# Key products of chunks 16 to 23 made ahead of the chunk loop, from inputs without block-diagonal copies

## The chip, the cores and the metric

The kernel runs on one core of one Trainium2 chip. The metric is the device time of one execution in microseconds. Before the change three executions took 909.39, 907.27 and 908.71 us, median 908.71 us. Below, PE is TensorE, DVE is VectorE, ACT is ScalarE, POOL is GpSimd and SP the engine that issues the DMAs.

## The reference, cut to what matters

Three layers follow one another: a delta-rule attention, a Fourier-mixing layer with an MLP, and a gated MLP. Only the attention is touched.

```python
def _attn_ref(q, k, v, beta):                 # (4, 8, 768, 48)
    k_n = k / (np.linalg.norm(k, axis=-1, keepdims=True) + 1e-06)
    state = np.zeros((B, H, D, D))
    for t in range(S):
        kt, vt, bt = k_n[:, :, t], v[:, :, t], beta[:, :, t, None]
        y[:, :, t] = np.einsum('bhd,bhde->bhe', q[:, :, t], state)
        v_old = np.einsum('bhde,bhd->bhe', state, kt)
        state = state + bt[:, :, :, None] * np.einsum('bhd,bhe->bhde', kt, vt - v_old)
```

## The kernel before, in words

The 768 steps are cut into chunks of C = 64, so that there are 48 pairs of batch and chunk (NBC = 48, numbered bc in the order in which they are worked on). A chunk covers 8 heads, held as 4 head pairs (HP) with one head on partitions 0 to 47 and the other on partitions 64 to 111. Eight chunks make a block (NB = 6 blocks).

For each chunk **stage_a** multiplies keys by queries and keys: the tile `kq` (112 x 4 x 256, 448 KB) holds, per head pair, 64 query columns, 64 key columns and 128 columns of keys once more, laid out block-diagonally, so that one whole-array matmul (L204) serves both heads. The products are evicted from a PSUM bank (tag X, 4 banks) into the ring tile `gak`. For chunks 8 to 15 ACT evicts in three instructions without the causal mask (L186, L187, L208); for chunks 16 on DVE evicts and masks in one (L210). Chunks 0 to 7 have a form of their own, `pairs0` (L178): keys and queries come without the block-diagonal copy, and each head is a matmul of 48 rows by 64 columns, one head in one corner of the array and one in the other.

**prep** (L233 to L243) builds from the key products of a block the triangular system that **solve** inverts on DVE (L253 to L308, mostly L287 and L292). `prep(blk + 1)` stands inside `solve(blk)` and waits in program order until stage_a has been recorded for the whole next block. For block 1 prep multiplies by a mask of its own (L238), since its products were evicted unmasked; `mask_q` (L220, L224) masks the query part of such chunks later, two chunks at a time.

The program has a **head** and a **chunk loop**. In the head: fills, 20 small warm-up matmuls (`busy`, L473, which compute nothing that is used), `pairs0` for keys, `solve(0)` on DVE, `pairs0` for queries, stage_a for chunks 8 to 15 each followed by one 512-column `busy` matmul (`keep`), then 8 more (`last`), `mask_q(0)` and `start(1)`, which is prep and root of block 1. The loop runs t from -3 to 47. Iteration t merges half-blocks of the inverse (`merge`, L359 and L362, 32x32 matmuls, evicted by ACT as `zs` and `TT`), and calls stage_b(t + 2) (L393, evicted into `WU`), stage_c(t + 1) (L409, then DVE's `cw`, L410) and stage_d(t) (L422, L424, then ACT's `Sb` and `x`). It also calls stage_a for a chunk 20 ahead (`ring`): chunks 16 and 17 at t = -3, 18 and 19 at t = -2 and -1, then t + 20. The instructions of `solve` are spread over eight iterations between those calls.

Instructions run in the order in which they are recorded on each engine; `chain` ties this order down. So an instruction that waits holds back all that follows on its engine, and the engines wait for each other in the order of the program.

Of the kernel before, what the change touches and what calls it, by code (L numbers as in the profile page):

```python
# [7 lines left out]
F32 = mybir.dt.float32  # L8
# [12 lines left out]
C = 64  # L21
NC = S // C
HP = H // 2
NBC = B * NC
# [3 lines left out]
GA = C + 2 * D  # L28
NT = B * S // 128

TOK = np.concatenate([np.arange(S // 2), [S // 2], S - np.arange(1, S // 2)])

MG = [(0, 97), (97, 193), (193, 289), (289, 384)]
# [8 lines left out]

CF = dict(
    skew=4, ring=20, kq=5, qt=3, mb=2, cvd=3, cve=2, kn=4, sv="hhhhhd", few=3,
    warm=20, keep=1, last=8, cuts=(0.5, 0.65), dfs=(1, 1, 1, 1, 2, 2, 3, 1, 1, 1, 2), cvt=(0, 0, 0, 0, 1, 1, 1, 1, 1, 1, 1), early=5,
    turns=(4, 5, 6, 7, 8, 9, 10, 11, 13, 14, 15, 16, 17, 17, 18, 19), stats=(((0, 1, 2, 3, 3), (2,)), ((20, 21, 22), (23, 24, 25))),
)

# [14 lines left out]
class Kernel:  # L63
# [36 lines left out]
    def load(self, out, in_):  # L100
        return self.nc.sync.dma_start(out=out, in_=in_)
# [13 lines left out]
    def attention(self, cp, pg, pe, p, x, filler, after_solves):  # L115
        nc, a, load = self.nc, self.a, self.load
# [12 lines left out]
        gas, Tts, st, kqs, qts, preps, seen_a = {}, {}, {}, {}, {}, {}, [0]  # L129
# [32 lines left out]
        def ring(bc):  # L162

            gak = (pe if bc // 4 % 6 < 3 else p).tile([128, 4, HP, GA], F32, name="gak", bufs=3)
            for i in range(4):
                gas[bc + i] = gak[:, i]
            gas[bc, 4] = gak


        ROWS = (slice(0, D), slice(0, C)), (slice(64, 64 + D), slice(64, 64 + C))  # L170
# [10 lines left out]
        def both0(i, at):  # L181
            return gas[i // 2 * 4, 4][:, i % 2 * 2 : i % 2 * 2 + 2, :, at : at + C].rearrange("p a b c -> p (a b) c")

        def copy_g(out, in_):

            nc.scalar.activation(out[:, :, :32], in_[:, :, :32], AF.Copy, scale=mk[:, 4 * C + 1 : 4 * C + 2])  # L186
            nc.scalar.copy(out=out[:, :, 32:], in_=in_[:, :, 32:])  # L187

        def mask_a(bc, n):
            m = 2 * C if SEQ[bc][1] < HALF else 0  # L190
            return mk[:, m : m + n].unsqueeze(1)

        def load_kq(bc):
            if 8 <= bc < NBC:
                kqs[bc] = pe.tile([112, HP, 4 * C], F32, name="kq", bufs=CF["kq"])
                load(out=kqs[bc], in_=a["kq"][bc])

        def stage_a(bc):
            kq = kqs.pop(bc)
            if bc % 4 == 0:  # L200
                ring(bc)
            pa = self.bank("pa", [128, HP, 2 * C])
            for hp in range(HP):
                nc.tensor.matmul(pa[:, hp], lhsT=kq[:, hp, 2 * C :], rhs=kq[:, hp, : 2 * C], start=True, stop=True)  # L204
            if bc < 16:

                copy_g(gas[bc][:, :, C : 2 * C], pa[:, :, C:])
                nc.scalar.copy(out=gas[bc][:, :, :C], in_=pa[:, :, :C])  # L208
            else:
                nc.vector.tensor_tensor(  # L210
                    out=gas[bc][:, :, : 2 * C], in0=pa, in1=mask_a(bc, 2 * C).to_broadcast([128, HP, 2 * C]), op=MUL
                )
            load_kq(bc + CF["kq"])
            seen_a[0] = bc + 1

        def mask_q(bc):
# [10 lines left out]
        def prep(blk):  # L227


            Cc = pe.tile([128, 1024], F32, name="Cc").rearrange("p (g c) -> p g c", g=32)  # L230
            for h4 in range(2):
                g4 = gas[blk * 8 + h4 * 4, 4][:, :, :, C : 2 * C].rearrange("p a b c -> p (a b) c")
                nc.vector.scalar_tensor_tensor(  # L233
                    out=Cc[:, h4 * 16 : h4 * 16 + 16], in0=g4[:, :, 32:], scalar=mk[:, 4 * C : 4 * C + 1], in1=g4[:, :, :32], op0=MUL, op1=ADD
                )
                yield 750
            if blk == 1:
                nc.vector.tensor_mul(Cc, Cc, mk[:, 4 * C + 2 : 4 * C + 34].unsqueeze(1).to_broadcast([128, 32, 32]))  # L238
                yield 1200

            Tf = pe.tile([128, 1056], F32, name="Ts", bufs=CF["mb"])
            T = Tf[:, :1024].rearrange("p (i j) -> p i j", i=32)
            nc.vector.transpose(out=T, in_=Cc.rearrange("p g c -> p c g"))  # L243
            preps[blk] = Tf, T
            yield 2000
# [85 lines left out]
        def start(blk):  # L331
            for _ in prep(blk):
                pass
            root(blk)
# [37 lines left out]
        def load_kv(bc):  # L372
            load(out=gas[bc][:, :, C:], in_=a["kv"][bc])
# [70 lines left out]
        for n in "kq":  # L444
            t = p.tile([128, 4, HP, GA], F32, name="gak", bufs=3).rearrange("p a b c -> p (a b c)")[:112, :2048]
# [4 lines left out]
                load(out=bt, in_=a["bt"])  # L450
                load(out=mk, in_=a["mk"])
        for i in range(CF["kq"]):
            load_kq(8 + i)
        load(out=qx, in_=a["qx"].rearrange("b p h -> p b h"))
        for i in range(2):
            load_qt(i)
# [11 lines left out]
        warm = TT[0].rearrange("p a b -> p (a b)")  # L468

        def busy(n, cols):  # L470
            wb = self.bank("pd", [128, cols])
            for i in range(n):
                nc.tensor.matmul(wb, lhsT=warm[:, :128], rhs=warm[:, :cols], start=True, stop=True)  # L473
# [8 lines left out]
        Spread(solve(0), 0).finish()  # L482
        for i in range(4):
            nc.scalar.copy(out=both0(i, 0), in_=pairs0("q", i))
        for bc in range(8, 16):
            stage_a(bc)
            busy(CF["keep"], 512)
        busy(CF["last"], 512)
        mask_q(0)
        start(1)  # L490
# [6 lines left out]
        R = CF["ring"]  # L497
        T0 = -3
        for t in range(T0, NBC):
            j, i = divmod(t + 11, 8)  # L500
            if i == 0 and j < NB:
                if solver:
                    solver.finish()
                solver = Spread(solve(j), 27600 if j < NB - 1 else 29000)
            part = (lambda f: solver.upto((i + f) / 8)) if j < NB else (lambda f: None)
            if light(t) and solver:
                solver.finish()
                solver = None

            if 0 <= t + 2 < NBC:  # L510
                values(t + 2)
            if t % 2 == 0 and 2 <= t + 2 < 16:
                mask_q(t + 2)
            part(c1)
            if t >= 0:
                stage_d(t)
                if SEQ[t][1] == NC - 1:
                    fill.extend(filler(SEQ[t][0]))
            new = t % 8 == 5 and t + 3 < NBC
            if new:  # L520

                merge((t + 3) // 2, True, False)
                load_kv(t + 3)
                load_kv(t + 4)
                diag((t + 3) // 2, up)
            if 0 <= t + 1 < NBC:
                stage_c(t + 1)
            part(c2)
            if t + R < NBC:
                if t >= 0:  # L530
                    stage_a(t + R)
            if t % 2:
                g = (t + 3) // 2
                if g < NBC // 2:
                    merge(g + 1, (g + 1) % 4 > 0, True)
                    if new:
                        diag(g, lo)
            elif t % 8 != 4 and t + 4 < NBC:
                diag((t + 4) // 2, up + lo)
            if (t + 4) % 8 > 1 and t + 4 < NBC:  # L540
                load_kv(t + 4)
            if light(t):

                for _ in range(CF["dfs"][t - (NBC - 11)]):
                    while fill and next(fill[0], 1) == 1:
                        fill.pop(0)
                for _ in range(CF["cvt"][t - (NBC - 11)]):
                    next(tail, None)
            if 0 <= t + 2 < NBC:
                stage_b(t + 2)  # L550
            if 2 <= t + 4 < NBC:
                load_qt(t + 4)
            if t < 0:
                for bc in range(16 if t == T0 else t + R, t + R + 1):
                    stage_a(bc)
            part(1)
            self.chain()
            if t == NBC - 12:
                loads, tail = after_solves()
            next(loads, None)  # L560
            self.chain()
# [536 lines left out]
def layout(q, k, v, beta, moe_w_ch1, moe_w_ch2, moe2_w_in, moe2_w_spatial, moe2_b_spatial, moe2_w_out):  # L1098
    f = np.float32
    o = {}  # L1100
# [11 lines left out]
    kq = np.zeros((B, NC, 2, 64, HP, 4, C), f)  # L1112
# [4 lines left out]
    kq = kq.reshape(NBC, 128, HP, 4 * C)[perm, :112]  # L1117
    o["kq"] = kq

    o["kq0"] = np.stack([kq[:8, :, :, C : 2 * C], kq[:8, :, :, :C]]).transpose(0, 2, 1, 3, 4)  # L1120

    qe = np.zeros((B, NC, 2, 64, HP, 112), f)
# [10 lines left out]
    j, i = (np.arange(128) % C)[:, None], np.arange(C)[None]  # L1133
# [7 lines left out]
    r = [np.arange(j, S // 2, 6)[None] for j in range(6)]  # L1141
# [39 lines left out]
    o["wi"] = rows(moe2_w_in)  # L1181
    o["ws"] = rows(moe2_w_spatial.T[np.ix_(TOK, TOK)])
    o["wo"] = rows(moe2_w_out)
    o["bs"] = moe2_b_spatial[TOK].reshape(1, S)
    return {n: np.ascontiguousarray(w) for n, w in o.items()}
# [19 lines left out]
```

## Time and profile before

| what | value |
|---|---|
| median of 3 executions | 908.71 us (907.27 to 909.39) |
| the profiled execution | 907.29 us, its span 905.5 us |
| busy PE / DVE / ACT | 863.4 us (95%) / 596.1 us (66%) / 392.0 us (43%) |
| chain that ended last, by engine | PE 72%, DVE 17%, ACT 8% |
| mean granted TensorE clock | 0.98 of full speed |

Busy shares are averages over the whole span. [...] The chain is followed back from the last instruction and says what each step waited for.

### The profile page before, as it was taken

The numbers are of one execution on the slowest core, as the hardware profiler recorded it, in microseconds if no ns is written. First come the engines' busy times: TensorE is split into PE (matmuls) and PEld (weight loads), VectorE is DVE, ScalarE is ACT, GpSimd is POOL, SyncE is SP. The second block draws the span as 40 slices with busy tenths as digits, with TensorE's granted clock in tenths as the row PEclk, the third lists the DMA queues.
The fourth block names the chain that finished last, engine by engine and source line by source line (L and its number), as shares of the span: only waits on it lengthen the run. The fifth ranks groups of instructions, "written<-read, shape, count | busy, mean of one in ns | idle before, by whom it ended". The sixth has DMA issues, their size and how long they took to land.

```text
span 905.5 us, 18349 instructions
## 1 busy us (share of the span) xinstructions
PE 863.4 (95%) x7115; PEld 826.0 (91%) x7115; DVE 596.1 (66%) x1796; ACT 392.0 (43%) x1004; POOL 71.2 (8%) x75
## 2 busy tenths in 40 slices
PE   7969999999999798999999999999999999999998
PEld 7668888998899688999999999999989999899898
DVE  5989999898875999678393694422385472452521
ACT  1265878788966544311212252221262251341412
POOL 2000000000000000000000000000023222222221
PEclk8988999999999999999999999999999999999999
DMA  7565565642354360000011511110132210000001
GB/s 213 163 164 130 147 183 155 167 133 72 90 152 128 97 234 1 1 1 11 17 46 52 167 27 27 27 27 18 31 110 70 73 34 27 28 1 27 27 1 54
DMA packets 58698, 70.88 MB, mean 78 GB/s; under 512 B 31953, under 2 KB 49074, under 8 KB 58610
## 3 DMA queue, kind: packets, MB, share of 16 engines
q1 hardware_dynamic: 58610, 69.70, 26.9%
q8 instruction: 56, 0.92, 0.4%
q14 instruction: 32, 0.26, 0.1%
HBM read 57.29 MB, written 4.72 MB: 68 GB/s over the span
## 4 chain that ended last, share of the span: by engine, by line
PE 72%; DVE 17%; ACT 8%; issue 2%; DMA 1%; POOL 0%; ACTq 0%; SPq 0%; DVEq 0%; POOLq 0%
PE bankX L791 15%; PE bankY L807 13%; PE bankX L930 11%; PE bankX L916 6%; PE bankY L950 6%; PE bankX L891 5%; DVE tm L287 2%; DVE Ts L292 2%; PE bankY L409 2%; ACT TT L348 2%; PE bankY L393 2%; ACT WU L398 2%; PE bankY L424 2%; PE bankX L612 2%; PE bankY L422 2%
## 5 line engine op out<-in xcount | busy, mean ns | idle before, releaser
L791 PE MATMUL bankX<-uh,w 128*128 128x384 f32 x504 | 136.8, 338 | 2.4 <-DVE ul L719 2.4
L807 PE MATMUL bankY<-w,hh 128*128 128x384 f32 x504 | 117.5, 339 | 1.1 <-DVE w L693 1.1
L799 DVE SCALAR_TENSOR_TENSOR hl<-bankX,hh 128x384 fp32r<-128x384 f32 x84 | 46.4, 552 | 97.2 <-ACT hh L798 97.2
L798 ACT ACTIVATE hh<-bankX 128x384 fp32r<-128x384 f32 x84 | 41.2, 491 | 156.9 <-PE bankX L791 154.6
L930 PE MATMUL bankX<-ws,vh 128*128 128x384 f32 x384 | 97.6, 336 | 0.0
L791 PEld LDWEIGHTS bankX<-uh,w 128*128 128x128 f32 x504 | 91.9, 188 | 3.1 <-DVE ul L719 2.9
L807 PEld LDWEIGHTS bankY<-w,hh 128*128 128x128 f32 x504 | 90.1, 188 | 2.2 <-DVE w L693 1.7
L791 PE MATMUL bankX<-ul,w 128*128 128x384 f32 x252 | 84.9, 337 | 0.0
L422 PE MATMUL bankY<-WU,gak 128*112 128x96 f32 (+1 forms) x384 | 70.2, 271 | 3.5 <-ACT x L439 3.2
L424 PE MATMUL bankY<-Sb,cw 112*112 112x96 f32 (+1 forms) x352 | 66.0, 271 | 7.9 <-DVE cw L410 6.4
L908 POOL TENSOR_TENSOR vl<-v,vh 128x512 fp32r<-128x512 f32 x24 | 31.9, 1335 | 519.1 <-DMA x<-un 442.4
L807 PE MATMUL bankY<-w,hl 128*128 128x384 f32 x252 | 72.1, 338 | 0.0
L930 PEld LDWEIGHTS bankX<-ws,vh 128*128 128x128 f32 x384 | 69.4, 188 | 0.0
L938 DVE TENSOR_TENSOR g<-bankX,bsb 128x384 f32<-128x384 f32 x32 | 17.7, 557 | 78.2 <-PE bankX L930 71.9
L930 PE MATMUL bankX<-ws,vl 128*128 128x384 f32 x192 | 63.7, 336 | 0.0
L292 DVE TENSOR_TENSOR Ts<-Ts,tm 128x110 f32<-128x110 f32 (+26 forms) x264 | 59.0, 261 | 0.8
L287 DVE TENSOR_TENSOR tm<-Ts 128x110 f32<-128x110 f32 (+26 forms) x264 | 58.7, 259 | 0.5
L424 PEld LDWEIGHTS bankY<-Sb,cw 112*112 112x112 f32 (+1 forms) x352 | 50.8, 184 | 8.5 <-issue 6.1
L422 PEld LDWEIGHTS bankY<-WU,gak 128*112 128x112 f32 (+1 forms) x384 | 54.2, 184 | 4.6 <-ACT x L439 4.3
L393 PE MATMUL bankY<-gak,TT 128*128 128x96 f32 x384 | 54.1, 286 | 3.2 <-issue 2.7
L393 PEld LDWEIGHTS bankY<-gak,TT 128*128 128x128 f32 x384 | 48.7, 198 | 5.2 <-issue 3.0
L916 PE MATMUL bankX<-xh,s 128*128 128x384 f32 x192 | 50.1, 338 | 1.4 <-ACT v L900 1.4
(179 smaller groups left out, 1858.8 us busy)
## 6 DMA issues: line engine op xcount, KB each, us to landing
kq<-in_kq_dram SPq DMA_DIRECT2D x40, 448.0 KB, 4.2
qt<-in_qt_dram SPq DMA_DIRECT2D x48, 196.0 KB, 3.9
gak<-in_kv_dram SPq DMA_DIRECT2D x48, 192.0 KB, 3.9
w<-in_w_dram SPq DMA_DIRECT2D x24, 384.0 KB, 7.5
x<-un SPq DMA_DIRECT2D x128, 36.0 KB, 1.9
out_dram<-ot SPq DMA_DIRECT2D x24, 192.0 KB, 2.0
s<-in_wi_dram SPq DMA_DIRECT2D x6, 512.0 KB, 4.5
un<-xh SPq DMA_DIRECT2D x80, 36.0 KB, 1.9
```

The lines of the kernel that those rows point to most:

```text
L287: nc.vector.tensor_tensor(out=tm, in0=T[:, r, k : k + 1].to_broadcast(sh), in1=T[:, k : k + 1, :k].to_broadcast(sh), op=MUL)
L292: nc.vector.tensor_add(o, o, tm)
L393: nc.tensor.matmul(pb[:, hp].rearrange("p t d -> p (t d)"), lhsT=tt[:, o + hp], rhs=kv[:, hp], start=True, stop=True)
L422: nc.tensor.matmul(pd[:m, hp], lhsT=ak[:, hp, :m], rhs=u[:, hp], start=True, stop=(c == 0))
L424: nc.tensor.matmul(pd[:m, hp], lhsT=cw[:, hp, :m], rhs=sb[:, hp], start=False, stop=True)
L791: nc.tensor.matmul(ph, lhsT=w1[f][i][:, c * 128 : c * 128 + 128], rhs=cur[k][:, c], start=(c + j == 0), stop=(c == 2 and j == 2))
L799: nc.vector.scalar_tensor_tensor(out=hl, in0=ph, scalar=0.0, in1=hh.bitcast(F32), op0=MAX, op1=SUB)
L807: nc.tensor.matmul(acc[t], lhsT=hx[i][:, t * 128 : t * 128 + 128], rhs=w2[e][k], start=(e == 0 and j == 0), stop=(e == 11 and j == 2),)
L891: nc.tensor.matmul(pv, lhsT=xT[t // 3][i][:, c, (t % 3) * 128 : (t % 3) * 128 + 128], rhs=wi[2 * c + 1][k], start=(c + j == 0), stop=(c == ...
L916: nc.tensor.matmul(pu, lhsT=wi[2 * c][i][:, f * 128 : f * 128 + 128], rhs=xT[hf][k][:, c], start=(c + j == 0), stop=(c == 2 and j == 2),)
L930: nc.tensor.matmul(pv, lhsT=vn[i][:, s, f * 128 : f * 128 + 128], rhs=ws[2 * s + hf][k], start=(s + j == 0), stop=(s == 5 and j == 2),)
L950: nc.tensor.matmul(po, lhsT=gt[i][:, f, t * 128 : t * 128 + 128], rhs=wo[f][k], start=(f + j == 0), stop=(f == 3 and j == 2),)
```

## The change

Chunks 8 to 23 (HEAD = 24) now all have their stage_a in the head. Their input is a new array `kc` without the block-diagonal copies: one `kq` tile of 448 KB holds two chunks. Each head pair is two matmuls of 48 rows by 64 columns (`ROWS`, as in `pairs0`) in place of one whole-array matmul. ACT evicts all of them unmasked. The `keep` matmuls are gone and `last` is 16 in place of 8. The loop's stage_a begins at t = 4 with chunk 24; the masks follow, for block 2's keys in `prep` (one multiplication of 128x1024) and for the queries of chunks 16 to 23 in `mask_q` at t = 14, 16, 18 and 20.

```diff
+HEAD = 24
-    warm=20, keep=1, last=8, ...
+    warm=20, keep=1, last=16, ...
         def load_kq(bc):
-            if 8 <= bc < NBC:
+            if bc < HEAD:
+                if 8 <= bc and bc % 2 == 0:
+                    t = pe.tile([112, HP, 4 * C], F32, name="kq", bufs=CF["kq"]).rearrange("p a n -> p (a n)")
+                    kqs[bc], kqs[bc + 1] = (t[:, i * HP * 2 * C : (i + 1) * HP * 2 * C].rearrange("p (a n) -> p a n", a=HP) for i in range(2))
+                    load(out=t.rearrange("p (c n) -> p c n", c=2), in_=a["kc"][:, bc - 8 : bc - 6])
+            elif bc < NBC:
...
             for hp in range(HP):
-                nc.tensor.matmul(pa[:, hp], lhsT=kq[:, hp, 2 * C :], rhs=kq[:, hp, : 2 * C], start=True, stop=True)
-            if bc < 16:
+                if bc < HEAD:
+                    for r, q in ROWS:
+                        nc.tensor.matmul(pa[q, hp], lhsT=kq[r, hp, C:], rhs=kq[r, hp], start=True, stop=True)
+                else:
+                    nc.tensor.matmul(pa[:, hp], lhsT=kq[:, hp, 2 * C :], rhs=kq[:, hp, : 2 * C], start=True, stop=True)
+            if bc < HEAD:
...
-            if blk == 1:
+            if blk in (1, 2):
                 nc.vector.tensor_mul(Cc, Cc, mk[:, 4 * C + 2 : 4 * C + 34].unsqueeze(1).to_broadcast([128, 32, 32]))
...
-        for bc in range(8, 16):
+        for bc in range(8, HEAD):
             stage_a(bc)
-            busy(CF["keep"], 512)
         busy(CF["last"], 512)
...
-            if t % 2 == 0 and 2 <= t + 2 < 16:
+            if t % 2 == 0 and 2 <= t + 2 < HEAD:
                 mask_q(t + 2)
...
-            if t + R < NBC:
-                if t >= 0:
-                    stage_a(t + R)
+            if HEAD <= t + R < NBC:
+                stage_a(t + R)
+            if t < T0 + CF["kq"]:
+                load_kq(HEAD + t - T0)
...
-            if t < 0:
-                for bc in range(16 if t == T0 else t + R, t + R + 1):
-                    stage_a(bc)
```

The order on PE from the program's start to the first stage_b, before the change; `TT` is the operand of the `busy` matmuls, `kq` the input of stage_a, bankZ what `merge` writes, and the row with bankY<-gak is the first stage_b:

```order
L473 MATMUL bankY<-TT_83 128x128 x20
L178 MATMUL bankX<-gak 64x64 x128
L204 MATMUL bankX<-kq 128x128 x4
L473 MATMUL bankY<-TT_83 128x512
...
L473 MATMUL bankY<-TT_83 128x512 x9
L359 MATMUL bankZ<-T_406,gak 32x32 x17
L362 MATMUL bankZ<-TT_83,zs 32x32
...
L204 MATMUL bankX<-kq 128x128 x8
L393 MATMUL bankY<-gak,TT_83 128x96 x4
```

The same place on PE with the change (line numbers are those of the changed kernel):

```order
L488 MATMUL bankY<-TT_83 128x128 x20
L180 MATMUL bankX<-gak 64x64 x128
L213 MATMUL bankX<-kq 64x128 x128
L488 MATMUL bankY<-TT_83 128x512 x16
L374 MATMUL bankZ<-T_406,gak 32x32 x17
L377 MATMUL bankZ<-TT_83,zs 32x32
...
L408 MATMUL bankY<-gak,TT_83 128x96 x4
```

Between the 128 small matmuls of `pairs0` and the first merge PE now has 128 more small matmuls and 16 `busy` matmuls in one piece, where it had 8 times 4 whole-array matmuls with a `busy` matmul behind each and 8 more at the end; the 8 matmuls of chunks 16 and 17 ahead of the first stage_b are gone.

The order on DVE at the end of `solve(1)` (t = 3 and 4), before the change; `T` and `Tc` are the inverse, `Cc` and the second `Ts` the system of block 2, `sq` its diagonal:

```order
L294 TENSOR_TENSOR Ts<-Ts,dT 128x1024
L410 TENSOR_TENSOR cw<-qt,bankY 112x448
L300 STREAM_TRANSPOSE T_1082<-Ts 128x512
L210 TENSOR_TENSOR gak<-bankX,mk 128x4x128
L300 STREAM_TRANSPOSE T_1082<-Ts 128x512
L410 TENSOR_TENSOR cw<-qt,bankY 112x448
L210 TENSOR_TENSOR gak<-bankX,mk 128x4x128
L233 SCALAR_TENSOR_TENSOR Cc<-gak,mk 128x512 x2
L243 STREAM_TRANSPOSE Ts<-Cc 128x1024
L220 TENSOR_TENSOR gak<-gak,mk 128x8x64
L308 STREAM_TRANSPOSE Tc<-Ts 128x16x32
L136 COPY sq<-Ts 128x32
```

The same place on DVE with the change:

```order
L309 TENSOR_TENSOR Ts<-Ts,dT 128x1024
L425 TENSOR_TENSOR cw<-qt,bankY 112x448
L315 STREAM_TRANSPOSE T_1154<-Ts 128x512 x2
L248 SCALAR_TENSOR_TENSOR Cc<-gak,mk 128x512 x2
L425 TENSOR_TENSOR cw<-qt,bankY 112x448
L253 TENSOR_TENSOR Cc<-Cc,mk 128x1024
L258 STREAM_TRANSPOSE Ts<-Cc 128x1024
L235 TENSOR_TENSOR gak<-gak,mk 128x8x64
L323 STREAM_TRANSPOSE Tc<-Ts 128x16x32
L221 TENSOR_TENSOR gak<-bankX,mk 128x4x128
L138 COPY sq<-Ts 128x32
```

The evictions of chunks 22 and 23 are gone, the mask of block 2's system has come in, and the eviction of chunk 24 stands one instruction earlier. The building of that system no longer comes behind the eviction of chunk 23.

## Rows read from the trace of the kernel before

**Rows 1.** The page's first line.

```profile
span 905.5 us, 18349 instructions
```

**Rows 2.** The chain that ended last, 43 to 72 us: start, length, step.

```profile
48.40 0.20 DVE sq L136
...
48.85 0.27 ACT zs L365
...
69.18 0.54 DVE cw L410
```

**Rows 3.** The timeline of PE: start, length, instructions, idle time before and its end.

```profile
7.99 5.58 PE L178 MATMUL bankX<-gak 48*64 48x64 f32 x183
16.55 4.21 PE L178 MATMUL bankX<-gak 48*64 48x64 f32 x73 [2.98 <-issue]
20.68 2.07 PE L204 MATMUL bankX<-kq 112*128 112x128 f32 x8
22.55 1.91 PE L473 MATMUL bankY<-TT 128*128 128x512 f32 x2
...
36.29 7.89 PE L473 MATMUL bankY<-TT 128*128 128x512 f32 x18
...
44.11 1.08 PE L359 MATMUL bankZ<-T,gak 32*32 32x32 f32 x32
...
51.02 3.78 PE L204 MATMUL bankX<-kq 112*128 112x128 f32 x16
...
60.96 0.96 PE L409 MATMUL bankY<-gak,WU 128*112 128x112 f32 x8
```

**Rows 4.** Stretches: length, busy PE, PEld, DVE, ACT, POOL; clock, DMA share, GB/s.

```profile
8.00:12.00 4.00, 4.00 (x137) 4.00 (x138) 2.09 (x4) 0.00 (x0) 0.00 (x0) 1.00 1.03 292
...
16.60:20.60 4.00, 4.00 (x73) 3.96 (x73) 3.79 (x16) 1.46 (x3) 0.15 (x1) 0.50 0.59 138
20.70:25.00 4.30, 4.30 (x15) 3.27 (x15) 4.30 (x31) 1.38 (x4) 0.00 (x0) 0.50 0.27 75
26.00:36.00 10.00, 10.00 (x58) 7.15 (x57) 10.00 (x57) 4.74 (x18) 0.00 (x0) 1.00 0.75 220
...
51.00:56.00 5.00, 5.00 (x27) 4.98 (x24) 2.57 (x9) 4.42 (x13) 0.15 (x1) 0.50 0.34 107
...
137.00:176.00 39.00, 36.87 (x534) 34.85 (x528) 36.07 (x139) 32.33 (x96) 0.16 (x1) 1.00 0.60 163
```

**Rows 5.** The timeline of ACT, 17 to 24 us.

```profile
19.08 0.58 ACT L484 COPY gak<-bankX 128x512 f32<-128x512 f32 x1 [1.12 <-PE bankX L178]
20.79 0.58 ACT L484 COPY gak<-bankX 128x512 f32<-128x512 f32 x1 [1.12 <-PE bankX L178]
22.79 0.37 ACT L186 ACTIVATE gak<-bankX,mk 128x128 f32<-128x128 f32 x1 [1.42 <-PE bankX L204]
...
23.20 0.39 ACT L208 COPY gak<-bankX 128x256 f32<-128x256 f32 x1
```

**Rows 6.** The timeline of DVE, 49 to 91 us.

```profile
53.13 0.69 DVE L210 TENSOR_TENSOR gak<-bankX,mk 128x512 f32<-128x512 f32 x1 [1.34 <-PE bankX L204]
54.84 0.69 DVE L210 TENSOR_TENSOR gak<-bankX,mk 128x512 f32<-128x512 f32 x1 [1.01 <-PE bankX L204]
...
83.72 0.62 DVE L410 TENSOR_TENSOR cw<-qt,bankY 112x448 f32<-112x448 f32 x1 [0.41 <-PE bankY L409]
...
90.08 0.15 DVE L136 COPY sq<-Ts 128x32 f32<-128x32 f32 x1
```

**Rows 7.** Single lines: count, shortest/median/longest ns, first and last start (L210: 40 to 92 us).

```profile
L210 DVE TENSOR_TENSOR gak<-bankX,mk x9: 651/685/692, 53.1 to 91.0; 128x512 f32<-128x512 f32 x9
L220 DVE TENSOR_TENSOR gak<-gak,mk x4: 645/680/685, 43.2 to 88.6; 128x512 f32<-128x512 f32 x4
L224 DVE TENSOR_TENSOR gak<-gak,mk x8: 386/420/424, 97.4 to 131.8; 128x256 f32<-128x256 f32 x8
L238 DVE TENSOR_TENSOR Cc<-Cc,mk x1: 1226/1226/1226, 45.2 to 45.2; 128x1024 f32<-128x1024 f32 x1
```

More of the change, by code (lines that the diff above doesn't have):

```diff
@@ L44 @@
     skew=4, ring=20, kq=5, qt=3, mb=2, cvd=3, cve=2, kn=4, sv="hhhhhd", few=3,
-    warm=20, keep=1, last=8, cuts=(0.5, 0.65), dfs=(1, 1, 1, 1, 2, 2, 3, 1, 1, 1, 2), cvt=(0, 0, 0, 0, 1, 1, 1, 1, 1, 1, 1), early=5,
+    warm=20, keep=1, last=16, cuts=(0.5, 0.65), dfs=(1, 1, 1, 1, 2, 2, 3, 1, 1, 1, 2), cvt=(0, 0, 0, 0, 1, 1, 1, 1, 1, 1, 1), early=5,
     turns=(4, 5, 6, 7, 8, 9, 10, 11, 13, 14, 15, 16, 17, 17, 18, 19), stats=(((0, 1, 2, 3, 3), (2,)), ((20, 21, 22), (23, 24, 25))),
@@ L212, in stage_a @@
                 )
-            load_kq(bc + CF["kq"])
+            if bc < HEAD:
+                if bc % 2 and bc + 2 * CF["kq"] < HEAD:
+                    load_kq(bc + 2 * CF["kq"] - 1)
+            else:
+                load_kq(bc + CF["kq"])
             seen_a[0] = bc + 1
@@ L452, in attention @@
         for i in range(CF["kq"]):
-            load_kq(8 + i)
+            load_kq(8 + 2 * i)
         load(out=qx, in_=a["qx"].rearrange("b p h -> p b h"))
@@ L1118, in layout @@
     o["kq"] = kq
+    o["kc"] = kq[8:HEAD, :, :, : 2 * C].transpose(1, 0, 2, 3).reshape(112, HEAD - 8, -1)
     o["kq0"] = np.stack([kq[:8, :, :, C : 2 * C], kq[:8, :, :, :C]]).transpose(0, 2, 1, 3, 4)
```

## The prediction

> **What bounds the kernel now.** I read the chain of waits first, then the timelines of PE, ACT and DVE up to 100 us, then the granted clock in the same stretches. In the chain the first 100 us belong to DVE: it ends solve(0), builds block 1's system, and its copy of the diagonal at 48.40 us lets ACT and then PE start the loop, with the first `zs` at 48.85 us; the chain returns to DVE until the first `cw` at 69.18 us [rows 2]. PE does its head work beside that and is not waited for: its last filler matmuls run from 36.29 us and the first merge is done at 45.19 us, 3.7 us before `zs` [rows 3]. The reader is to see how thin this cover is, and the clock with it. PE's small two-corner matmuls of `pairs0` run at a clock of 1.00 from 8 to 12 us; PE is then idle for 2.98 us before 16.55, and goes on at 0.50 [rows 3, 4]. From 16.6 to 20.6 us it is busy without a gap with these small matmuls and the clock stays at 0.50; then whole-array matmuls follow, the clock is still 0.50 up to 25 us and 1.00 from 26 us [rows 4].
>
> **The head with the change: PE.** All is as before up to 20.7 us, where stage_a of chunk 8 begins: the queue has loads of the same sizes up to there. Then come 16 chunks of eight small matmuls, and 16 filler matmuls of 512 columns.
>
> One chunk: 8 matmuls of 128 columns are as many columns as a group of `pairs0`, 16 matmuls of 64. At the clock of 0.50 such a group took 20.79 - 19.08 = 1.71 us, by the evictions that waited for it [rows 5]. At 1.00, 183 records took 5.58 us, two records to a matmul, so 32 records, a group, 0.98 us [rows 3]. ACT is no limit: a chunk's three evictions take from 22.79 to 23.59 us, 0.80 us [rows 5]. Loads are none either: each 448 KB now serves two chunks, and only the last three wait for a tile to come free.
>
> [...]
>
> Which clock? This decides the forecast. Nothing ahead of 20.7 us changes, so the clock is at 0.50 there. Before, whole-array matmuls began at 20.68 us and the clock rose between 25 and 26 us; I take 4.8 us of them. Now the small matmuls go on instead. Four microseconds of them without a gap did not raise the clock [rows 4]; they fill two corners of 48 by 64 of the array. After the first merges, 32 by 32 matmuls, whole-array ones began at 51.02 us and the clock was still 0.50 at 56 us [rows 3, 4]. So in both places it was the whole-array matmuls that brought it up, some 5 us after they began. I forecast that it stays at 0.50 through all 16 chunks.
>
> Then stage_a ends at 20.7 + 16 x 1.71 = 48.1 us, where it ended at 36.3 us before. One filler matmul takes 7.89 us / 9 = 0.88 us at 1.00 [rows 3] (18 records, two to a matmul), and so 1.75 us at half the clock. In 4.8 us at 0.50 PE does 2.7 of them; the other 13.3 take 11.7 us: they end at 48.1 + 4.8 + 11.7 = 64.6 us. The first merge takes 1.1 us more: 65.7 us. The cover is gone, for DVE had released this point by 48.85 us, and all of ACT's loop work stands behind that first `zs`.
>
> **From the first merge to the first `cw`.** Before, from `zs` at 48.85 us to the end of stage_c's matmuls for it at 60.96 + 0.96 = 61.92 us it was 13.1 us [rows 2, 3]. The stage_a of chunks 16 and 17 (3.78 us, [rows 3]) is gone from it, but ACT worked meanwhile, so that little of it was on this path; some matmuls there ran at 0.50. I take 12.4 us, between 13.1 and 11.6 (0.6 us less for those chunks, 0.9 for the clock). So `cw` can begin at 65.7 + 12.4 = 78.1 us, 8.9 us later than 69.18.
>
> DVE is there early. In this stretch it loses four evictions of 0.68 us [rows 7] and the waits of 1.34 and 1.01 us ahead of the first two [rows 6]: 5.1 us, so it arrives at 64.1 us and waits 14 us for PE. The gain that the change makes on DVE is swallowed by this wait. Queued behind `cw` on DVE is the rest of solve(1), which is what sets the pace.
>
> **From there to the end of solve(1).** Between `cw` and the copy `sq` at 90.08 us four more evictions go (2.7 us) and a wait of 0.41 us [rows 6], while block 2's mask adds 1.23 us [rows 7]: 1.9 us less, if PE and ACT keep up, else nothing less. So `sq` is at + 7.0 us. Behind it the loop goes as before, in the order of the program, and nothing in it waits for a fixed time; the shift stays to the end.
>
> **The masks later.** At t = 14 to 20 DVE gets two multiplications of 0.68 us and four of 0.42 us, 3.0 us [rows 7]. From 137 to 176 us it is idle for 39.0 - 36.1 = 2.9 us of 39 [rows 4]. Either bound is possible, nothing (hidden in the gaps) or all 3.0; ACT and PE are the busier ones in the chain there, so I take 1.0 us. The loads of chunks 24 to 28 come earlier than they are needed and cost nothing.
>
> **Sum.** The profiled execution took 907.29 us (its span of 905.5 us [rows 1] and 1.8 us around it), 1.4 us under the median of 908.71. 907.3 + 7.0 + 1.0 = 915.3 us. Bounds of the unknowns: the clock's rise after 4.3 to 5.3 us of whole-array matmuls (25 and 26 us less 20.7), at half a microsecond for each, -0.3 to +0.3; the path to `cw` -0.8 to +0.7; ACT and PE keeping up, 0 to +1.9; the masks -1.0 to +2.0. Together 913 to 920 us for this case.
>
> **The rivals.**
> First, the clock rises during the small matmuls, as it did before, at 25.5 us. Then 2.8 chunks are done by 25.5 us, 13.2 take 12.9 us to 38.4, the fillers 14.1 us to 52.5, the merge to 53.6, and `cw` can begin at 66.0 us: 3.2 us early, just behind DVE's own 64.1. With the 1.9 us gained on DVE and the 1.0 for masks it gives 903.2 us, faster. For it speaks that the small matmuls at least did not lower the clock from 8 to 12 us [rows 4]. [...] Against it the trace has the 4 us without a gap at 0.50. Chance 0.16.
> Second, the clock rises half way, near 36 us, with nine chunks done: the other seven take 6.9 us, the fillers end at 57.0, `cw` begins at 70.5 us, + 1.3, and with - 1.9 and + 1.0 it comes to 907.7 us, no change. This is the point from which the sign turns: a rise before it is a gain, later a loss. Chance 0.06.
> Third, the two corners do not run side by side: a chunk then takes 3.4 us, stage_a ends at 75.1 us, the fillers at 91.6, the merge at 92.7, `cw` begins 36 us late, and it gives some 942 us. Against it stand the 0.98 and 1.71 us above. Chance 0.03.
>
> **How the numbers follow.** My case has 0.75. About 0.2% (1.8 us) is what can be told from no change. Faster: the first rival, 0.16. Same: the second and a little of mine, 0.07. Slower: the rest, 0.77. Predicted is my case, 915.3 us, with 913 to 920 us as its own range. The range for 8 times in 10 also takes in the second rival and the upper part of the first, and above half a microsecond for the distance of a median from a profiled execution: 903 to 920.5 us.
>
> **What would show it right or wrong.** Right: the granted clock at 0.50 from 16 us to past 50 us, 16 chunks at 1.7 us each, fillers from 48 us, a wait of DVE for PE of more than 10 us ahead of its first `cw`, ACT idle up to 65 us, and from 100 us on a constant shift. Wrong in the first step: a clock of 1.00 from some 26 us, stage_a over at 38 us, no such wait. Wrong in the later steps: the shift at `sq` is not that at `cw` less 2 us, or it goes on growing from 140 to 180 us, where the masks are.

## The result and the profile after

The changed kernel takes 899.99 us (median of 4 runs, 899.85 to 900.92) against 907.99 us of the kernel before on the same chip (4 runs, 907.0 to 909.39): ratio 0.9913, 95% interval 0.9896 to 0.993. It is faster by 8.0 us; the same kernel measured once more gained 6.3 us (a_again, below). I had forecast 915.3 us, slower, with a range from 903.0 us up: wrong in sign, and outside the range. The outcome is that of the first rival (903.2 us, chance 0.16), and 3 us better than it.

The page of the changed kernel begins with these lines: the span, then busy time, share and instructions of each engine.

```profile
span 898.1 us, 18625 instructions
...
PE 860.3 (96%) x7243; PEld 822.8 (92%) x7243; DVE 594.2 (66%) x1795; ACT 398.5 (44%) x1028; POOL 71.2 (8%) x75
```

Busy times differ by 2 to 6.5 us from those of before; what changed is the order of waits in the first 100 us. The timeline of PE after, which answers to [rows 3]:

```profile
17.32 4.21 PE L180 MATMUL bankX<-gak 48*64 48x64 f32 x73 [3.17 <-issue]
21.22 15.23 PE L213 MATMUL bankX<-kq 48*64 48x128 f32 x256
36.39 14.00 PE L488 MATMUL bankY<-TT 128*128 128x512 f32 x32
50.32 1.08 PE L374 MATMUL bankZ<-T,gak 32*32 32x32 f32 x32
...
63.66 0.97 PE L424 MATMUL bankY<-gak,WU 128*112 128x112 f32 x5
```

All 16 chunks are over at 36.4 us, not at the 48.1 us of my case, and the fillers at 50.4 us, not at 64.6. The first merge ends at 51.4 us, and the matmuls for the first `cw` at 63.66 + 0.97 = 64.63 us. The reason is the clock. Stretches after (columns as in [rows 4]: length, busy PE, PEld, DVE, ACT, POOL; clock, DMA share, GB/s):

```profile
18.00:20.00 2.00, 2.00 (x44) 2.00 (x42) 1.90 (x5) 0.73 (x2) 0.15 (x1) 0.50 1.03 231
20.00:22.00 2.00, 2.00 (x37) 2.00 (x35) 2.00 (x16) 0.88 (x2) 0.00 (x0) 0.50 0.18 60
22.00:24.00 2.00, 2.00 (x28) 2.00 (x26) 2.00 (x15) 0.88 (x4) 0.00 (x0) 0.66 0.00 0
24.00:26.00 2.00, 2.00 (x42) 2.00 (x39) 2.00 (x14) 1.66 (x7) 0.00 (x0) 1.00 0.42 70
...
55.00:64.00 9.00, 7.29 (x93) 6.99 (x94) 9.00 (x50) 8.28 (x26) 0.00 (x0) 0.50 1.09 254
137.00:176.00 39.00, 36.75 (x551) 34.83 (x550) 36.69 (x125) 30.62 (x90) 0.16 (x1) 1.00 0.63 165
```

PE has nothing but small matmuls from 17.32 to 36.4 us, and its clock goes from 0.50 to 1.00 in the middle of them, between 22 and 24 us. From then a chunk takes 0.87 us, by ACT's first eviction of each: behind the one at 24.27 us 14 more follow at this pitch; the first two and the last stand here. Below them is ACT's first `zs`.

```profile
24.27 0.37 ACT L188 ACTIVATE gak<-bankX,mk 128x128 f32<-128x128 f32 x1 [0.20 <-PE bankX L213]
25.14 0.37 ACT L188 ACTIVATE gak<-bankX,mk 128x128 f32<-128x128 f32 x1
...
36.50 0.37 ACT L188 ACTIVATE gak<-bankX,mk 128x128 f32<-128x128 f32 x1
...
51.45 0.38 ACT L380 ACTIVATE zs<-bankZ 128x256 f32<-128x256 f32 x1 [1.95 <-PE bankZ L374]
```

So `zs` is some 2.6 us later than before [rows 2] and waits 1.95 us for PE. It costs nothing, as the timeline of DVE shows (it answers to [rows 6]):

```profile
49.04 0.19 DVE L138 COPY sq<-Ts 128x32 f32<-128x32 f32 x1
...
64.78 0.61 DVE L425 TENSOR_TENSOR cw<-qt,bankY 112x448 f32<-112x448 f32 x1
...
83.60 0.66 DVE L221 TENSOR_TENSOR gak<-bankX,mk 128x512 f32<-128x512 f32 x1
84.19 0.16 DVE L138 COPY sq<-Ts 128x32 f32<-128x32 f32 x1
87.37 0.61 DVE L425 TENSOR_TENSOR cw<-qt,bankY 112x448 f32<-112x448 f32 x1
...
93.85 0.61 DVE L425 TENSOR_TENSOR cw<-qt,bankY 112x448 f32<-112x448 f32 x1
```

No bracket stands behind these `cw`: DVE comes from its own work each time. PE had the first one's operand ready at 64.63 us, 0.15 us before DVE took it. The chain of waits after says the same, it stays on DVE through the whole stretch (start, length, step):

```profile
47.05 1.97 DVE Ts L258
...
50.58 1.24 DVE Ts L268
...
64.87 0.53 DVE cw L425
...
79.04 1.15 DVE Cc L253
```

Where the gain comes from, by DVE's rows of both traces. The first `sq` is 0.64 us late (49.04 against 48.40 us [rows 2]). That is no part of the change: in all twelve traces of this document the first `sq` comes 40.35 to 40.49 us behind the start of `pairs0`, and this start differs from one execution to the next, from 7.78 to 9.27 us; it is 8.58 us here and 7.99 us before [rows 3]. From `sq` to the first `cw` it takes 15.74 us against 20.70 (69.10 - 48.40): 4.96 us less, four evictions of 0.68 us and the waits of 1.34 and 1.01 us [rows 6, 7]. From `cw` to the second `sq` 19.41 against 20.98 us: 1.57 less. Four evictions and waits of 0.41 and 0.28 us are gone there; block 2's mask and the eviction of chunk 24 (at 83.60 us above, behind `sq` before) have come in. At the next two `cw` the gain grows from 5.9 us to 6.4 and 7.9, for these are the rows of before, the first `cw` on top:

```profile
69.10 0.62 DVE L410 TENSOR_TENSOR cw<-qt,bankY 112x448 f32<-112x448 f32 x1
...
93.75 0.61 DVE L410 TENSOR_TENSOR cw<-qt,bankY 112x448 f32<-112x448 f32 x1
101.74 0.62 DVE L410 TENSOR_TENSOR cw<-qt,bankY 112x448 f32<-112x448 f32 x1 [1.45 <-PE bankY L409]
```

The first 0.5 us are the eviction of chunk 24 again, which before stands between `sq` and the `cw` at 93.75 us. Behind it, DVE waits 1.45 us for PE before, whose clock is 0.62 on the mean of this stretch:

```profile
96.50:101.00 4.50, 4.50 (x33) 4.42 (x28) 3.79 (x25) 3.76 (x12) 0.00 (x0) 0.62 0.28 85
```

After, it is 1.00 in that stretch, and the wait is gone. But only some 0.4 us of the wait belong to the kernel before: in h16 and b_last16 below, which are like it behind the head, the clock is 1.00 there, and DVE waits 0.40 and 0.38 us. The other 1.0 us is a low clock in the one profiled execution of before.

### The profile page after: what moved, and what is told of

Same layout as the page of the kernel before. It is cut to its first block, busy times and chain, and to the rows that moved or that the text cites. A ratio compares the mean times of both kernels' runs of the same rounds, so it can differ in the third digit from the quotient of the medians.

```text
span 898.1 us, 18625 instructions
## 1 busy us (share of the span) xinstructions
PE 860.3 (96%) x7243; PEld 822.8 (92%) x7243; DVE 594.2 (66%) x1795; ACT 398.5 (44%) x1028; POOL 71.2 (8%) x75
## 4 chain that ended last, share of the span: by engine, by line
PE 71%; DVE 21%; ACT 5%; issue 2%; POOL 0%; DMA 0%; SPq 0%; ACTq 0%; DVEq 0%; POOLq 0%
PE bankX L803 15%; PE bankY L819 13%; PE bankX L942 11%; PE bankX L928 6%; PE bankY L962 6%; PE bankX L903 5%; DVE tm L302 4%; DVE Ts L307 4%; PE bankY L424 2%; PE bankY L439 2%; PE bankX L624 2%; PE bankY L437 2%; PE bankY L408 2%; PE bankV L819 1%; PE bankX L640 1%
## 5 line engine op out<-in xcount | busy, mean ns | idle before, releaser
L439 PEld LDWEIGHTS bankY<-Sb,cw 112*112 112x112 f32 (+1 forms) x352 | 48.6, 177 | 4.1 <-DVE cw L425 3.2
```

Source lines behind the costliest of these rows:

```text
L439: nc.tensor.matmul(pd[:m, hp], lhsT=cw[:, hp, :m], rhs=sb[:, hp], start=False, stop=True)
```

## The experiments

Theory D: the gain is DVE's alone. It loses eight evictions with their waits, and PE's head work is hidden as long as PE has the operand of the first `cw` before DVE gets there. The rivals to it: F, the longer filler makes the gain; I, the inputs without copies make it possible, with the old ones the same work would not fit ahead; H, the later masks are hidden; D', relieving DVE is enough, wherever the products are made.

The table shows by how much ACT's `x` eviction of iteration t starts later (+) or earlier (-) than in the kernel before, in us, each from one profiled execution of that kernel. It is worked out from the starts of these evictions.

```
 t (before)     after  a_last32  a_last8  a_wide_last8  a_nomask  b_act  a_pool
 0 ( 62.1 us)   +2.33   +16.42    -0.58       +9.97       +3.54   +4.57   +1.74
 1 ( 73.5 us)   -4.31    +9.78    -6.51       +3.33       -3.11   -0.89   -2.37
 3 ( 84.2 us)   -6.08    +8.01    -7.36       +1.57       -4.88   -0.75   -2.53
 6 (101.7 us)   -8.45    +5.41    -9.30       -0.99       -7.07   -2.11   -5.59
12 (134.0 us)   -7.90    +5.95    -8.76       -0.45       -7.20   -1.54   -3.25
20 (175.6 us)   -6.53    +7.33    -7.37       +0.93       -7.20   -0.17   -1.46
33 (239.5 us)   -6.53    +7.35    -7.35       +0.94       -7.06   -0.19   -1.41
47 (310.6 us)   -7.82    +6.20    -6.22       -0.34       -8.16   -1.29   -2.69
```

At t = 34 all but a_last8 get 1.3 us from something that is no part of the change: PE's clock is 0.57 on the mean of 240 to 244 us in the kernel before, and 1.00 in the changed one, and in h16 and b_last16 too. The shifts also hold the start of each execution. `pairs0` began at 7.99 us in the kernel before and, in the order of the table, at 8.58, 8.65, 7.78, 8.88, 9.24, 9.27 and 8.11 us. Less this difference the changed kernel is 7.1 to 7.2 us ahead at t = 20 in all four of its traces with 8, 12 or 16 fillers (after, a_last8, a_again and a_last12).

**a_last32: the changed kernel with twice the filler.** It puts the end of PE's head work where my prediction had it.

```diff
-    warm=20, keep=1, last=16, ...
+    warm=20, keep=1, last=32, ...
```

> The changed kernel with 32 filler matmuls at the head's end in place of 16. Theory D (the gain is DVE's, which loses eight evictions and its waits for PE; the head's PE work is hidden only up to the point where DVE reaches its first cw at 64.8 us): the fillers end near 64.4 us, where my prediction had put them, the first zs comes at 65.5 us, the first cw about 13 us later, and the time is 911 to 915 us. Rival F (the longer filler is itself the gain, since it keeps TensorE's clock up into the loop): 16 more cost at most what the first zs is late beyond slack in the loop, 900 to 906 us.

Measured: 914.29 us (913.85 to 915.17), ratio 1.0070 (1.0055 to 1.0085), slower. Its timelines of PE, ACT and DVE:

```profile
36.75 27.73 PE L488 MATMUL bankY<-TT 128*128 128x512 f32 x64
64.41 1.07 PE L374 MATMUL bankZ<-T,gak 32*32 32x32 f32 x32
...
65.53 0.38 ACT L380 ACTIVATE zs<-bankZ 128x256 f32<-128x256 f32 x1 [16.01 <-PE bankZ L374]
...
78.62 0.62 DVE L425 TENSOR_TENSOR cw<-qt,bankY 112x448 f32<-112x448 f32 x1 [13.72 <-PE bankY L424]
...
98.03 0.18 DVE L138 COPY sq<-Ts 128x32 f32<-128x32 f32 x1
```

This is the trace that I had described: fillers over at 64.5 us (forecast 64.6), `cw` at 78.6 us (78.1), DVE's wait 13.7 us (14), `sq` 7.95 us late (7.0), time 914.3 us (915.3). D is right, and what I had worked out behind the clock holds as far as `sq`, of whose 7.95 us 0.66 us are the later start. Behind it the shift does not stay as I had said: it is 5.41 us at t = 6, 7.33 us at t = 20 and 6.20 us at the end (table), so that the forecast total is so near by luck in part.

**a_last8: the changed kernel with the filler of before.**

```diff
-    warm=20, keep=1, last=16, ...
+    warm=20, keep=1, last=8, ...
```

> The changed kernel with 8 filler matmuls at the head's end as before. Theory D: the fillers end near 43.4 us, the first zs comes 2 us earlier, DVE still sets the pace up to the first cw, so 899 to 901.5 us, whatever the clock does in the first merges. Rival F: half of the gain or more is lost, 904 to 908 us.

Measured: 901.18 us (900.37 to 901.85), ratio 0.9924 (0.9909 to 0.9939). F falls: without the longer filler the gain is there. The first `zs` comes at 48.53 us with no wait for PE, and the clock is 0.50 from about 46 to 62 us. Still DVE needs 15.74 us from `sq` to `cw` (48.17 to 63.91 us), exactly as in the changed kernel. That its loop runs 0.8 us ahead up to t = 33 is no merit of the fillers: this execution began 0.80 us earlier (`pairs0` at 7.78 against 8.58 us).

**b_last16: the kernel before with the longer filler.**

```diff
-    warm=20, keep=1, last=8, ...
+    warm=20, keep=1, last=16, ...
```

> The kernel before with 16 filler matmuls in place of 8 at the head's end, nothing else. Theory D: the first zs is some 3.4 us later and the evictions of chunks 16 and 17 with it, partly made good by a higher clock: 907 to 911 us. Rival F: a good part of the change's gain shows, 901 to 905 us.

Measured: 908.85 us (907.62 to 911.15, 10 runs), ratio 1.0015 (1.0004 to 1.0027). F falls here too: `zs` is at 52.27 us after a wait of 3.30 us for PE, `cw` at 70.81 us, 1.7 us late, and nothing is gained.

**a_wide_last8: a_last8 with the old inputs and whole-array matmuls in the head.**

```diff
-            if bc < HEAD:
...
-                    load(out=t.rearrange("p (c n) -> p c n", c=2), in_=a["kc"][:, bc - 8 : bc - 6])
-            elif bc < NBC:
+            if 8 <= bc < NBC:
...
-                if bc < HEAD:
-                    for r, q in ROWS:
-                        nc.tensor.matmul(pa[q, hp], lhsT=kq[r, hp, C:], rhs=kq[r, hp], start=True, stop=True)
-                else:
-                    nc.tensor.matmul(pa[:, hp], lhsT=kq[:, hp, 2 * C :], rhs=kq[:, hp, : 2 * C], start=True, stop=True)
+                nc.tensor.matmul(pa[:, hp], lhsT=kq[:, hp, 2 * C :], rhs=kq[:, hp, : 2 * C], start=True, stop=True)
...
-                if bc % 2 and bc + 2 * CF["kq"] < HEAD:
-                    load_kq(bc + 2 * CF["kq"] - 1)
+                if bc + CF["kq"] < HEAD:
+                    load_kq(bc + CF["kq"])
...
-            load_kq(8 + 2 * i)
+            load_kq(8 + i)
```

> The changed kernel with 8 fillers, and stage_a of chunks 8 to 23 in the head from the old block-diagonal inputs: whole-array matmuls, a 448 KB load for each chunk instead of for two. Theory D: only where the evictions stand matters; if the loads keep up with about 1.6 us each, stage_a ends near 45 us, the fillers near 52, and the time is 899 to 902 us. Rival I (the inputs without copies are what makes it possible, since the loads would hold the head back): stage_a ends after 48 us and the time is over 903 us.

Measured: 905.33 us (902.16 to 907.2, 10 runs), ratio 0.9964 (0.9949 to 0.9979): 4 us of the 6.3 us that a_last8 gained over the same runs of before (907.52 us) are lost. I is right, and the 899 to 902 us of D were missed. PE's stage_a now waits for loads; PE and DVE in the timelines:

```profile
33.26 1.16 PE L206 MATMUL bankX<-kq 112*128 112x128 f32 x8 [2.19 <-DMA kq<-in_kq_dram]
...
46.22 4.67 PE L206 MATMUL bankX<-kq 112*128 112x128 f32 x24 [2.01 <-DMA kq<-in_kq_dram]
50.68 7.34 PE L479 MATMUL bankY<-TT 128*128 128x512 f32 x16
...
72.22 0.62 DVE L416 TENSOR_TENSOR cw<-qt,bankY 112x448 f32<-112x448 f32 x1 [4.98 <-PE bankY L415]
```

Its loads from 20 to 52 us, by the view of DMA issues (count, KB each, median us to landing):

```profile
kq<-in_kq_dram SPq DMA_DIRECT2D x11, 448.0 KB, 7.5
```

In the changed kernel there are three of that size behind 20 us, at a median of 4.4 us. stage_a ends at 50.9 us against 36.4, and DVE waits 4.98 us ahead of the first `cw`, which is what it had saved. The two waits for loads are 4.2 us of the 14.5 us by which stage_a ends later. PE also works at a clock of 0.50 up to 27.4 us, from 35 to 41 and from 48 to 51 us. The run changes the inputs and the kind of matmul at once, so the share of each is not shown.

**a_nomask: the changed kernel without the new masks.** It leaves out block 2's key mask and the query masks of chunks 16 to 23.

```diff
-            if blk in (1, 2):
+            if blk == 1:
...
-            if t % 2 == 0 and 2 <= t + 2 < HEAD:
+            if t % 2 == 0 and 2 <= t + 2 < 16:
```

> The changed kernel without the masks that it adds: block 2's key mask and the query masks of chunks 16 to 23 are left out. Theory D: the key mask of 1.23 us stands on DVE's path at the end of solve(1), and the four query masks cost 1.4 us (the shift of the loop fell from 7.9 to 6.5 us between t = 18 and t = 20): 897 to 898 us. Rival H (the masks are hidden in DVE's idle time): 899.5 to 900.5 us.

Measured: 898.43 us (897.97 to 898.95), ratio 0.9896 (0.9878 to 0.9914). The median, 1.6 us under that of the changed kernel, lies between the two expectations (it is 2.8 us under a_again). Its loop began later: `sq` at 49.73 and `cw` at 65.96 us, 0.7 and 1.2 us behind. In the places of the masks it is plain. From `cw` to the second `sq` it takes 17.57 us against 19.41, but some 0.6 us of this are the eviction of chunk 24, which here comes behind `sq`:

```profile
83.53 0.16 DVE L138 COPY sq<-Ts 128x32 f32<-128x32 f32 x1
...
84.47 0.67 DVE L221 TENSOR_TENSOR gak<-bankX,mk 128x512 f32<-128x512 f32 x1
```

From the first `cw` to the `cw` behind `sq`, with that eviction inside in both, it takes 21.27 us against 22.59: 1.32 us less. And there is no shift from t = 12 to 20, where the changed kernel loses 1.37 us (table). So the key mask costs about its 1.23 us [rows 7], the query masks about half of their 3.0 us, and H falls.

**b_act: the kernel before, with ACT evicting chunks 16 to 23 where they were, in the loop.**

```diff
-            if bc < 16:
+            if bc < 24:
...
-            if blk == 1:
+            if blk in (1, 2):
...
-            if t % 2 == 0 and 2 <= t + 2 < 16:
+            if t % 2 == 0 and 2 <= t + 2 < 24:
```

> The kernel before with one part of the change: chunks 16 to 23 are evicted by ACT unmasked and masked later on DVE, but their stage_a stays in the loop. Theory D' (DVE's relief is enough, wherever the products are made): 900 to 903 us. Theory D (the evictions have to leave the loop's start, where ACT is busy too and each eviction holds back zs, TT and WU behind it): 8 times 0.8 us more on ACT take the gain back, 905 to 910 us.

Measured: 906.46 us (904.86 to 908.51, 10 runs), ratio 0.9989 (0.9979 to 0.9998). D is right, D' falls. DVE's timeline has its relief turned into waits for PE:

```profile
66.64 0.62 DVE L410 TENSOR_TENSOR cw<-qt,bankY 112x448 f32<-112x448 f32 x1 [1.17 <-PE bankY L409]
...
72.17 0.62 DVE L410 TENSOR_TENSOR cw<-qt,bankY 112x448 f32<-112x448 f32 x1 [0.75 <-PE bankY L409]
...
82.98 0.62 DVE L410 TENSOR_TENSOR cw<-qt,bankY 112x448 f32<-112x448 f32 x1 [2.88 <-PE bankY L409]
```

PE still makes the products between the loop's matmuls, and ahead of L409 it waits for ACT's `WU`, behind which ACT's new evictions stand; by the view of waits from 50 to 90 us (us in total, times, longest):

```profile
PE bankY L409 <- ACT WU L398: 2.2, 2, 1.1
```

Products and evictions stay in the loop together here, so this run does not tell which of the two takes the relief back.

**h16: the kernel before with the new inputs and small matmuls for chunks 8 to 15 only.** Fillers, evictions and the matmuls of chunks 16 on are as before; the loads of chunks 16 to 20 follow as tiles come free.

```diff
-            if 8 <= bc < NBC:
+            if bc < 16:
...
+                    load(out=t.rearrange("p (c n) -> p c n", c=2), in_=a["kc"][:, bc - 8 : bc - 6])
+            elif bc < NBC:
...
-                nc.tensor.matmul(pa[:, hp], lhsT=kq[:, hp, 2 * C :], rhs=kq[:, hp, : 2 * C], start=True, stop=True)
+                if bc < 16:
+                    for r, q in ROWS:
+                        nc.tensor.matmul(pa[q, hp], lhsT=kq[r, hp, C:], rhs=kq[r, hp], start=True, stop=True)
+                else:
+                    nc.tensor.matmul(pa[:, hp], lhsT=kq[:, hp, 2 * C :], rhs=kq[:, hp, : 2 * C], start=True, stop=True)
```

> The kernel before with the new inputs alone: stage_a of chunks 8 to 15 as two small matmuls per head pair from inputs without block-diagonal copies, fillers and loop as before. Theory D: the head's PE work stays hidden behind solve(0), no change, 906.5 to 908.5 us. A rival in which fewer bytes or the earlier rise of TensorE's clock is the gain: 900 to 904 us. Where the clock rises in this run tells besides whether small matmuls raise it sooner than whole-array ones (4.6 to 6.0 us after they began against 8.8 to 9.5 so far).

Measured: 908.45 us (907.54 to 911.18, 10 runs), ratio 1.0013 (1.0002 to 1.0024): no gain from the inputs alone, as D has it. It also serves as the test of the clock by itself, since the head differs from before in the kind of matmul and its loads only: see below.

**a_pool: the changed kernel with the loop's query masks on GpSimd.** It was to take these masks off DVE.

```diff
-                nc.vector.tensor_tensor(out=out, in0=out, in1=m, op=MUL)
+                (nc.vector if bc == 0 else nc.gpsimd).tensor_tensor(out=out, in0=out, in1=m, op=MUL)
```

> The changed kernel with the loop's query masks (chunks 2 to 23) on GpSimd in place of DVE. Theory D (DVE sets the pace up to t = 6 and partly at t = 18 to 20): DVE loses seven times 0.68 us or so, 2 us of the three masks up to t = 4 and the 1.4 us at t = 18 to 20 come off, 896 to 898.5 us. Rival: GpSimd needs about 1.3 us for each and stage_b or stage_d waits for it, or it slows DVE down: 900 us or more.

Measured: 904.45 us (903.05 to 907.36, 10 runs), ratio 0.9971 (0.9958 to 0.9985). The expectation of D is missed by 6 us. GpSimd's and DVE's timelines of this kernel, and then DVE's of the changed one at the same step:

```profile
51.54 3.71 POOL L235 TENSOR_TENSOR gak<-gak,mk 128x512 f32<-128x512 f32 x3
...
51.36 4.32 DVE L280 SCALAR_TENSOR_TENSOR Ts<-Ts 128x30 f32<-128x30 f32 x6
```

```profile
51.84 1.30 DVE L280 SCALAR_TENSOR_TENSOR Ts<-Ts 128x30 f32<-128x30 f32 x6
```

The same six instructions take 4.32 us beside GpSimd's masks, and 1.30 us without them: three of them last 1.21 to 1.30 us, as long as one of GpSimd's masks (1.27 us), the others 0.26 to 0.27 us. From `sq` to `cw` it is 18.17 us against 15.74. The work was off DVE, the time was not.

**a_again and a_last12: the changed kernel once more, and with `last=12`.**

> The changed kernel once more, unaltered, beside the next one on the same chip: 899.5 to 901 us by any theory.

> The changed kernel with 12 filler matmuls in place of 16. Theory D: the fillers end near 47 us, the first merge near 48, ahead of DVE's release at 49.3 us, so the first zs comes 2 us earlier than in the changed kernel; DVE sets the pace anyway and at most 1 us is won in the loop (8 fillers had the loop 0.85 us ahead): 898.5 to 900.5 us. Rival F (the fillers pay by holding the clock up): 900.5 to 903 us.

Measured: a_again 901.21 us (899.53 to 901.99, 6 runs), ratio 0.9922 (0.9908 to 0.9937); a_last12 900.46 us (899.45 to 901.37, 6 runs), ratio 0.9917 (0.9902 to 0.9932). The intervals overlap almost wholly, with that of a_last8 too: fillers of 8, 12 and 16 can't be told apart, and no version better than the changed kernel is shown. a_last12 is as D has it; a_again is 0.2 us above its expectation.

**The clock in these runs.** Up to chunk 8 PE has the same instructions in all of them: 73 records of `pairs0`, begun at a clock of 0.50 (in b_act 0.4 us before the clock fell to it). Then either small matmuls go on, or whole-array ones follow some 4 us later. Stretches from 22 to 26 us, first h16 (small, begun at 18.15 us):

```profile
22.00:24.00 2.00, 2.00 (x24) 1.83 (x21) 2.00 (x16) 0.66 (x2) 0.00 (x0) 0.60 0.02 8
24.00:26.00 2.00, 2.00 (x19) 1.07 (x19) 2.00 (x14) 0.72 (x3) 0.00 (x0) 1.00 0.01 4
```

then a_wide_last8 (whole-array, begun at 17.85 us):

```profile
22.00:24.00 2.00, 2.00 (x10) 2.00 (x10) 2.00 (x16) 0.59 (x1) 0.00 (x0) 0.50 0.00 0
24.00:26.00 2.00, 2.00 (x12) 2.00 (x11) 2.00 (x14) 0.99 (x4) 0.00 (x0) 0.50 0.41 117
```

In all eight traces in which small matmuls go on (in h16 with fillers between), the clock is 1.00 by 25 us, between 21.7 and 24.8 us; in the four with whole-array ones it rises between 24.8 and 27.4 us. So the clock does rise with PE at small matmuls, and no later than at the others. Why it comes later with whole-array matmuls, these runs don't tell.

## Why the prediction was wrong

**What bounds the kernel, and the cover.** Right: DVE sets the first 100 us, and PE's head work costs nothing up to the point at which DVE wants the first `cw`. After, that point is at 64.78 us and PE is ready at 64.63.

**The clock: the step that failed.** "I forecast that it stays at 0.50 through all 16 chunks." It rose in their first 3 us. I had two observations for it. The first, that 4 us of small matmuls without a gap did not raise the clock [rows 4], was no evidence: by my own working whole-array matmuls needed 4.8 us for it, and at 51.02 us more than 5 [rows 3, 4]. The stretch of small ones was shorter than either, so it could not show that they were different: in the changed kernel PE had done nothing but small ones from 17.32 us to past 22 us when the clock rose. The second, that the rise came during whole-array matmuls, only says what happened to be next in the program. A row speaks against a mechanism only if by the other one it would have looked different; these rows would have been the same. The trace after has what the first rival says, 0.50 to 1.00 between 22 and 24 us in nothing but 48 by 64 matmuls, and I had set that rival aside for a row that did not bear on it. In the sum the step is the 16 x 1.71 us of stage_a at half the clock and the fillers begun at it: 48.1 and 64.6 us, where the runs have 36.4 and 50.4 us.

**What stands behind the clock.** Right as far as `sq`, as a_last32 shows with the fillers' end brought to the forecast place. Its terms, forecast and measured there: from the end of the first merge to `cw` 12.4 us against 78.62 - 65.48 = 13.1 us, the upper bound that I gave.

**The first rival's sum.** Its mechanism came, with terms off by little. The clock rose before 24 us, not at 25.5. A chunk at 1.00 takes 0.87 us, not 0.98; a filler 14.00 / 16 = 0.875 us, as worked out. The fillers end at 50.4 us, not 52.5, and `cw` is at 64.78, not 66.0 us, set by DVE, which I had at 64.1. The relief of DVE up to `cw` is 4.96 us, forecast 5.1; between `cw` and `sq` 1.57 us, forecast 1.9: the sum left out the eviction of chunk 24, which now stands ahead of `sq`, and the wait of 0.28 us.

**"Behind it the loop goes as before."** Wrong by some 2 us: from `sq` to the second `cw` behind it the gain grows from 5.9 to 7.9 us. Of this 0.5 us are the eviction of chunk 24, and 1.45 us a wait of DVE for PE, of which some 1.0 us is the low clock of that one execution. The wait was in the trace of before, at 101 us, and the prediction counts no wait behind the last evictions. With the 1.3 us at t = 34, some 2.3 us of the gain between the two profiled executions are chance in that of before. How often its other executions have such a low clock is not shown; the medians are 8.0 and 6.3 us apart in two measurements.

**The masks later.** I took 1.0 us between 0 and 3.0; 1.37 us are lost from t = 18 to 20, and nothing in a_nomask. The mask of block 2's system, which I had charged at its 1.23 us, costs 1.3 us (21.27 against 22.59 us).

**The third rival,** heads one after the other, did not come: 16 chunks took 15.23 us. At a clock of 1.00 the 1024 columns of a chunk take 0.87 us, as long as the 512 columns of a filler (0.875 us), so the two corners run side by side.

## What to carry to other kernels

Where a forecast hangs on a state (a clock, a queue, a cache), ask of each row whether it would look different under the rival, and count a stretch that is too short to show the state's change as no evidence. Work taken off the bounding engine is worth its length only if what the engine waits for next is early enough: here taking eight evictions off DVE gained 6 to 8 us with the products made ahead from small inputs, 2.2 us with whole-array matmuls on inputs of twice the size, 1.1 us with products and evictions left in the loop, and 6.8 us were lost when 16 more filler matmuls stood ahead. Before two traces are compared in tenths of a microsecond, take off what differs before the change can act: here the start of `pairs0`, by up to 1.5 us. Before moving work to an idle engine, look whether the busy one slows down beside it: here six instructions of DVE took 4.32 us beside GpSimd's masks, and 1.30 us without them.

## What the hardware showed that I had not expected

TensorE's granted clock went from 0.50 to 1.00 while PE had nothing but small matmuls that fill two 48 by 64 corners of the array (in the changed kernel 0.66 on the mean of 22 to 24 us, 1.00 from 24 to 36 us), and in these runs no later than with a stage of whole-array matmuls that begins 4 us in (between 21.7 and 24.8 us against 24.8 to 27.4 us).

PE ran at 0.50 from 55 to 64 us in the changed kernel, while DVE had 9.00 of 9.00 us of work: half the clock cost nothing there, and a_last8 with 16 us of it was no slower (901.18 us against 901.21 us of a_again).

DVE's SCALAR_TENSOR_TENSOR took longer beside GpSimd's multiplications in a_pool: 4.32 us for six instructions against 1.30 us in the changed kernel. Three of the six last 1.21 to 1.30 us, as long as a GpSimd mask (1.27 us), the others 0.26 to 0.27 us. What holds DVE up there, no run shows.
